# Grouped-query attention on one core: the first queries in one transposed load, all plain loads of the first groups at the top

## The chip, the cores and the metric

One NeuronCore of a Trainium2 chip runs the whole problem. The metric is the device time of the execution in microseconds, the median over several executions.

## The reference

```python
B, Hq, Hkv, Sq, Sk, D = 16, 32, 8, 288, 512, 128          # bf16, q, k, v ~ 0.05 * normal

def reference(q, k, v):
    k = jnp.repeat(k, rep, axis=1); v = jnp.repeat(v, rep, axis=1)      # rep = 4
    scores = jnp.einsum("bhqd,bhkd->bhqk", q, k) * D ** -0.5
    p = softmax(scores, axis=-1)
    return jnp.einsum("bhqk,bhkd->bhqd", p, v)
```

## The kernel before

There are 128 groups (batch times key head). Each has 1152 query rows (nine tiles of 128), 512 keys, and three **rounds**, so 384 rounds. A round's scores are 1536 columns of PSUM in three blocks of 512 (the kernel's `BANK`): TensorE makes the transposed scores, ScalarE takes the exponential, TensorE multiplies with the values two rounds later, VectorE divides. Scores and exponentials alternate between two halves of PSUM.

Queries and most keys come by transposed loads that SyncE issues. For a quick start the keys of groups 0 and 1 come by plain loads that ScalarE issues and are transposed on TensorE; the queries of group 0 come in two transposed loads, of four and five tiles.

```python
def op_q0(i):                                   # two loads: tiles 0..3 and 4..8
    c0, c1 = ((0, TB), (TB, NT))[i]
    nc.sync.dma_start_transpose(qt_sb[:, 0, c0:c1], q_v[0:P, c0 * D:c1 * D]).then_inc(sem["s_qp%d" % i], 16)

def have_q(g, i):
    if g == 0:
        return ("s_qp%d" % min(i, 1), 16)       # round 0: first half; rounds 1, 2: second half
    ...

first = [lambda i=i: op_q0(i) for i in range(2)]
first += [lambda: op_q(1), lambda: op_k(0, 2), lambda: op_v(0, None, 1, UG), lambda: op_q(2), lambda: op_q(3)]

@block.tensor
def _(eng):
    op_warm(WARM, BANK, ps_o[:, 1])             # WARM = 5 dummy matmuls of 512 columns
    op_warm(1, P, ps_o[:, 1])
    op_kt(0, range(1), 0)                       # transposes of group 0's keys
    op_kt(0, range(1, NJ), 1)
    op_warm(1, P, ps_s[:, 1])
    for n in range(NS):
        op_s(n)                                 # scores of round n
        if shared(n):
            op_sy(n)
        if n == 2:
            op_kt(1, range(NJ), 1)              # transposes of group 1's keys
        if n >= LAG:
            op_pv(n - LAG)                      # values of round n - 2
    ...

@block.scalar
def _(eng):
    op_kd(eng, 0)                               # keys of group 0
    eng.activation(dum[:], nc.const_aps.tensor(0.0, [P, 1], FP32), ACTF.Exp)     # fetches the table (1.28 us)
    for (s, n) in need(eng, [("s_kd0", 16)]):
        eng.wait_ge(s, n)                       # until they have landed
    op_v(0, eng, 0, 1)                          # values of group 0
    op_kd(eng, 1)                               # keys of group 1
    for n in range(NS):
        op_exp(n)                               # rounds 0 and 1 in three pieces of 512 columns
    ...
```

In every sixth round (`shared`) the last 120 columns of the exponential are computed on VectorE.

## Time and profile before

| | before |
|---|---|
| time, median of 3 | 522.29 us (522.13, 522.29, 523.44) |
| span of the profiled execution | 521.9 us, and that execution took 523.58 us |
| TensorE / ScalarE busy | 99% / 98% |
| first half of group 0's queries | issued 0.82, landed 3.6 us |
| second half | issued 2.20, landed 6.53 us |
| first exponential of round 0 / 1 | 4.42 / 7.22 us |
| scores of round 3 begin | 10.35 us |

Read it from the head: what happens after round 3 is a gap-free stream, so the start of that stream, plus a constant, is the time.

### The profile page before, as it was taken

How to read it: one execution, taken by the hardware profiler on the slowest of the kernel's cores; microseconds unless marked ns; L12 is line 12 of the kernel's file. 1: busy time of each engine (PE TensorE's matmuls, PEld its weight loads, DVE VectorE, ACT ScalarE, POOL GpSimd, SP SyncE). 2: the span in 40 equal slices, each digit the busy share in tenths (PEclk: the TensorE clock that was granted, in tenths of full speed). 3: DMA queues.
4: the chain of work that ended last, by engine and by line, in shares of the span. 5: the costliest groups of instructions: out<-in, count | busy, mean ns of one | idle time of the engine just before them, and what ended most of it. 6: DMA issues, size and time to landing. Idle time of an engine off the chain costs nothing.

```text
span 521.9 us, 15338 instructions
## 1 busy us (share of the span) xinstructions
PE 517.0 (99%) x6223; PEld 395.2 (76%) x6223; DVE 368.2 (71%) x1307; ACT 513.7 (98%) x393; POOL 79.8 (15%) x135
## 2 busy tenths in 40 slices
PE   8999999999999999999999999999999999999997
PEld 4777777777777777777777777777777777777776
DVE  1777677677677777776776766767767777677675
ACT  6999999999999999999999999999999999999997
POOL 2111111111111111111111111111111111111110
PEclk9999999999999999999999999999999999999999
DMA  8999999999999999999999989999999999998212
GB/s 181 243 228 234 217 209 217 245 208 232 224 219 270 187 251 200 229 257 226 224 229 239 179 233 231 226 202 193 218 248 232 214 215 195 197 244 183 91 69 92
DMA packets 253110, 110.06 MB, mean 211 GB/s; under 512 B 219760, under 2 KB 236784, under 8 KB 253040
## 3 DMA queue, kind: packets, MB, share of 16 engines
q1 hardware_dynamic: 252608, 108.69, 97.2%
q8 instruction: 49, 0.80, 0.6%
q10 hardware_dynamic: 432, 0.39, 0.3%
q14 instruction: 21, 0.17, 0.1%
HBM read 17.04 MB, written 37.75 MB: 105 GB/s over the span
## 4 chain that ended last, share of the span: by engine, by line
ACT 97%; PE 1%; DMA 1%; issue 1%; DVE 0%; SPq 0%
ACT pt_sb L514 96%; DMA qt_sb<-in_q_dram 1%; PE ps_s L437 1%; SPq L316 0%; ACT pt_sb L509 0%; PE ps_o L477 0%; DVE o_sb L583 0%; PE ps_o L404 0%; DVE o_sb L593 0%; PE ps_s L477 0%; DVE rl_sb L573 0%; PE ps_o L667 0%; DVE bad_sb L619 0%; DVE flag_i L733 0%; DVE bad_sb L616 0%
## 5 line engine op out<-in xcount | busy, mean ns | idle before, releaser
L514 ACT ACTIVATE pt_sb<-ps_s 128x1536 bf16<-128x1536 f32 (+2 forms) x384 | 509.2, 1441 | 0.9 <-PE ps_s L437 0.9
L477 PE MATMUL ps_o<-v_sb,pt_sb 128*128 128x129 bf16 x4584 | 322.2, 220 | 0.0
L477 PEld LDWEIGHTS ps_o<-v_sb,pt_sb 128*128 128x128 bf16 x4584 | 283.0, 98 | 49.7 <-DVE o_sb L583 13.7
L437 PE MATMUL ps_s<-qt_sb,kt_sb 128*128 128x512 bf16 (+2 forms) x1536 | 310.9, 325 | 1.3 <-DMA qt_sb<-in_q_dram 1.3
L583 DVE TENSOR_TENSOR o_sb<-ps_o,rl_sb 128x384 bf16<-128x384 f32 x382 | 211.9, 555 | 9.3 <-DVE rl_sb L573 0.5
L437 PEld LDWEIGHTS ps_s<-qt_sb,kt_sb 128*128 128x128 bf16 x1536 | 124.1, 98 | 64.1 <-DMA qt_sb<-in_q_dram 2.5
L573 DVE RECIPROCAL rl_sb<-ps_o 128x3 f32<-128x3 f32 x382 | 68.0, 178 | 126.8 <-PE ps_o L477 125.3
L566 POOL COPY v_sb<-vd_sb 128x512 bf16<-128x512 bf16 x128 | 78.9, 616 | 430.9 <-PE ps_o L477 418.7
L547 DVE SCALAR_TENSOR_TENSOR u_sb<-u_sb,m_sb 128x120 f32<-128x120 f32 x124 | 35.1, 283 | 2.1
L554 DVE SCALAR_TENSOR_TENSOR pt_sb<-u_sb,e_sb 128x120 bf16<-128x120 f32 x62 | 17.5, 283 | 2.2
L547 DVE SCALAR_TENSOR_TENSOR u_sb<-m_sb 128x120 f32<-128x120 f32 x62 | 17.1, 276 | 0.0
L525 DVE TENSOR_SCALAR y_sb<-ps_o 128x120 f32<-128x120 f32 x62 | 15.7, 253 | 0.0
L538 DVE TENSOR_SCALAR m_sb<-t_sb 128x120 int32<-128x120 int32 x62 | 13.8, 223 | 2.1
L448 PE MATMUL ps_o<-qt_sb,kt_sb 128*128 128x120 bf16 x62 | 13.4, 216 | 0.0
L538 DVE TENSOR_SCALAR e_sb<-t_sb 128x120 int32<-128x120 int32 x62 | 13.4, 216 | 0.0
L531 DVE TENSOR_SCALAR t_sb<-y_sb 128x120 int32<-128x120 f32 x62 | 13.2, 212 | 0.0
L448 PEld LDWEIGHTS ps_o<-qt_sb,kt_sb 128*128 128x128 bf16 x62 | 6.1, 98 | 7.3
L411 DVE COPY kt_sb<-ps_o 128x128 bf16<-128x128 bf16 (+2 forms) x3 | 1.0, 336 | 8.2 <-PE ps_o L404 8.1
L509 ACT ACTIVATE pt_sb<-ps_s 128x512 bf16<-128x512 f32 x6 | 3.3, 627 | 2.9 <-PE ps_s L437 2.9
L609 DVE TENSOR_REDUCE st_sb<-rl_sb 128x1 f32<-128x72 f32 (+1 forms) x16 | 3.5, 216 | 0.0
L611 DVE TENSOR_REDUCE st_sb<-rl_sb 128x1 f32<-128x72 f32 (+1 forms) x16 | 3.5, 216 | 0.0
L417 PE MATMUL ps_o<-const-bfloat16-1.0 128*128 128x512 bf16 (+1 forms) x6 | 2.4, 573 | 0.9 <-PEq L751 0.9
(32 smaller groups left out, 12.5 us busy)
## 6 DMA issues: line engine op xcount, KB each, us to landing
out_dram<-o_sb SPq DMA_DIRECT2D x127, 288.0 KB, 3.8
vd_sb<-in_v_dram SPq DMA_DIRECT2D x31, 512.0 KB, 5.3
qt_sb<-in_q_dram SPq DMA_TRANSPOSE x129, 5.0
kt_sb<-in_k_dram SPq DMA_TRANSPOSE x32, 5.0
vd_sb<-in_v_dram SPq DMA_DIRECT2D x1, 384.0 KB, 3.9
out_dram<-o_sb SPq DMA_DIRECT2D x3, 96.0 KB, 1.6
kd_sb<-in_k_dram ACTq DMA_DIRECT2D x2, 128.0 KB, 2.8
vd_sb<-in_v_dram ACTq DMA_DIRECT2D x1, 128.0 KB, 2.4
```

The costliest lines, as they stand in the source:

```text
L437: ins = emit(eng, w_x, lambda: eng.matmul(ps_s[:, n % 2, c:c + w], kt_sb[:, sl, j, gi, :], qg[:, t * P:t * P + w], start=True, stop=True))
L448: emit(eng, [("s_ev", n - LAG - 1)], lambda: eng.matmul(ps_o[:, (n - LAG) % 2, BANK - W:BANK], kt_sb[:, (g // UG) % NSLOT, j, g % UG, :], ...
L477: ins = emit(eng, w_x, lambda: eng.matmul(outs(r)[:, t - r % NC * TPC, :], pt(g, t, j), v_sb[:, sl, gi * NJ + j, 0:DV], start=(x == 0), st ...
L514: emit(eng, waits, lambda: eng.activation(d, s, ACTF.Exp, scale=scale)).then_inc(sem["s_e"], 1)
L525: emit(eng, [("s_yb", nth(n) - NB), ("s_pv", n - LAG + 1)], lambda: eng.tensor_scalar(out=y_sb[:, b], in0=ps_o[:, (n - LAG) % 2, BANK - W: ...
L531: emit(eng, [("s_ym", 2 * (nth(n) - NB)), ("s_y", nth(n))], lambda: eng.tensor_scalar(out=t_sb[:, b], in0=y_sb[:, b], scalar1=Y_MUL, scala ...
L538: emit(eng, [("s_yp", nth(n) - NB), ("s_yb", nth(n))], lambda: eng.tensor_scalar(out=dst[:, b], in0=t_sb[:, b], scalar1=mask, scalar2=bits ...
L547: lambda: eng.scalar_tensor_tensor(out=u_sb[:, b, x], in0=src, scalar=QUARTIC[x], in1=m, op0=ALU.add, op1=ALU.mult)
L554: lambda: eng.scalar_tensor_tensor(out=pt_sb[:, n % NPT, CH - W:CH], in0=u_sb[:, b, 2], scalar=QUARTIC[3], in1=e_sb[:, b].bitcast(FP32), o ...
L566: emit(eng, waits, lambda: eng.tensor_copy(v_sb[:, sl, gi * NJ:(gi + 1) * NJ, 0:D], vd_sb[:, sl, gi].rearrange("p (j d) -> p j d", d=D))). ...
L573: emit(eng, [("s_pv", r + 1)], lambda: eng.reciprocal(rl_sb[:, TPC * r:TPC * (r + 1)].unsqueeze(2), outs(r)[:, :, D:DV])).then_inc(sem["s_ ...
L583: emit(eng, waits, lambda: eng.tensor_tensor(out=o_sb[:, g % NO, t0:t0 + TPC, :], in0=outs(r)[:, :, 0:D], in1=rl_sb[:, TPC * r:TPC * (r + ...
```

## The change

The intent is a shorter head: one issue on SyncE less, so that the queries of group 1 follow at once, and no wait on ScalarE ahead of its second and third load.

```diff
-            c0, c1 = ((0, TB), (TB, NT))[i]
+            c0, c1 = 0, NT
...
-                return ("s_qp%d" % min(i, 1), 16)
+                return ("s_qp0", 16)
...
+                if n == 1 and x < 2:
+                    w_x = [have_q(g, x)]
...
-            return FIRST_SHARED <= n < NS - 6 and (n - FIRST_SHARED) % EVERY == 0
+            return FIRST_SHARED <= n < NS - NC and (n - FIRST_SHARED) % EVERY == 0
...
-        first = [lambda i=i: op_q0(i) for i in range(2)]
+        first = [lambda: op_q0(0)]
...
-        sp.append((NS - 2 + LAG + 2.5, op_stored))
+        sp.append((NS - NC + LAG + 2.5, op_stored))
...
-                if n == 2:
+                if n == 1:
                     op_kt(1, range(NJ), 1)
...
             op_kd(eng, 0)
-            eng.activation(dum[:], nc.const_aps.tensor(0.0, [P, 1], FP32), ACTF.Exp)
-            for (s, n) in need(eng, [("s_kd0", 16)]):
-                eng.wait_ge(s, n)
             op_v(0, eng, 0, 1)
             op_kd(eng, 1)
+            eng.activation(dum[:], nc.const_aps.tensor(0.0, [P, 1], FP32), ACTF.Exp)
```

NC is 3, so the new limit in `shared` adds one shared round, number 378. The transposes of group 1's keys move from behind scores 2 to behind scores 1.

## The prediction

> **What bounds the kernel now.** I read the engine shares of the page first, then busy time by stretches, then the order of time on TensorE, then the chain that ended last for the first 20 us. The page puts the chain on ScalarE (96% of the span in the exponentials), but two engines are nearly full there:
>
> ```profile
> PE 517.0 (99%) x6223; PEld 395.2 (76%) x6223; DVE 368.2 (71%) x1307; ACT 513.7 (98%) x393; POOL 79.8 (15%) x135
> ```
>
> The busy time of stretches (columns: PE, PEld, DVE, ACT, POOL, granted clock, DMA share, GB/s) and the order of time in the middle decide which one leads:
>
> ```profile
> 200.00:300.00 100.00, 100.00 (x1219) 76.96 (x1218) 73.14 (x262) 100.00 (x77) 15.51 (x26) 1.00 1.08 229
> ...
> 31.63 0.81 PE L437 MATMUL ps_s<-qt_sb,kt_sb 128*128 128x512 bf16 x3
> 32.28 0.84 PE L477 MATMUL ps_o<-v_sb,pt_sb 128*128 128x129 bf16 x12
> 32.96 0.82 PE L437 MATMUL ps_s<-qt_sb,kt_sb 128*128 128x512 bf16 x6
> ```
>
> The reader is to see starts, not lengths, because matmuls overlap: scores to values 0.65 us, values to the next scores 0.68 us, so 1.33 us for one of the 384 rounds, without a gap. ScalarE keeps up by a hair. Every sixth round its exponential is 120 columns short because VectorE computes them. While that goes on, its durations stay between 1390 and 1477 ns; after the last such round (502.1 us) they creep up, which I read as a queue building:
>
> ```profile
> L514 ACT ACTIVATE pt_sb<-ps_s x7: 1390/1452/1477, 29.8 to 37.8; 128x1536 bf16<-128x1536 f32 x6, 128x1416 bf16<-128x1416 f32 x1
> ...
> L514 ACT ACTIVATE pt_sb<-ps_s x11: 1391/1478/1540, 502.1 to 515.4; 128x1536 bf16<-128x1536 f32 x10, 128x1416 bf16<-128x1416 f32 x1
> ```
>
> So from about 11 us to 515 us TensorE's stream has no slack and nothing in this change shortens it. All that can move is the head and a little of the tail. The chain of the head:
>
> ```profile
> 0.82 1.32 SPq L316
> 2.14 0.06 issue
> 2.20 4.33 DMA qt_sb<-in_q_dram
> 6.53 0.05 issue
> 6.57 2.74 PE ps_s L437 x9
> 9.31 0.43 PE ps_o L404 x4
> 9.74 0.70 PE ps_o L477 x12
> 10.44 0.73 PE ps_s L437 x3
> ```
>
> The end of the time is set by the second half of the queries of group 0: issued at 2.20, landed at 6.53. The first half lets round 0 run (3.79 to 5.2), then TensorE sits idle for 1.34 us. Since no slack follows, each microsecond taken off this head comes off the total.
>
> [...] (1) [...] a 512-column matmul lasts 634 ns at most in the head and 379 ns in the middle, starts 0.43 us apart there and 0.215 us (0.65/3) here; the fast spacing comes at about 9.5 us, 3.0 us after TensorE became busy without a gap. The granted-clock column shows 1.00 in both and does not tell them apart. (2) [...] loads issued by different engines share the same 16 DMA engines. The trace agrees: in 4.5 to 5.0 us the queue of ScalarE's loads takes 86.5% of them and the queue of SyncE's transposes 7.5%. (3) [...] SyncE's queue moved 0.17 MB from 3 to 5 us, about all of its 0.16 MB, yet it landed only at 6.53, when ScalarE's loads (issued 3.07 and 3.44) were still draining. [...]
>
> ```profile
> L437 PE MATMUL ps_s<-qt_sb,kt_sb x9: 314/607/634, 6.6 to 9.0; 128*128 128x512 bf16 x5, 128*128 128x128 bf16 x4
> ...
> L437 PE MATMUL ps_s<-qt_sb,kt_sb x25: 219/379/379, 30.7 to 38.7; 128*128 128x512 bf16 x15, 128*128 128x128 bf16 x8, 128*128 128x392 bf16 x2
> ...
> q10 hardware_dynamic: 151, 0.14, 86.5%
> q1 hardware_dynamic: 49, 0.00, 7.5%
> ```
>
> **The change, part by part.**
>
> *One transposed load for group 0.* Removed: one issue of about 1.3 us on SyncE. The nine-tile issues of the other groups take 1391 to 1857 ns, median 1639, hardly more than four or five tiles (1319, 1255). So the single issue runs from 0.82 to about 2.45, and everything behind it in SyncE's queue comes 2.20 + 1.25 - 2.45 = 1.0 us sooner. In the kernel before, bytes began to flow when an issue was about over (second half: issue over at 3.45, first bytes at about 3.55), so I put them at 2.5.
>
> *Plain loads without the wait.* ScalarE's three loads go out at 0.82, about 1.25 and about 1.6 instead of 0.82, 3.07, 3.44. Their bytes (3 x 131 KB = 0.39 MB) start at 1.8 as the first does now, and compete with the 0.295 MB of queries. Both queues at their best moved 0.14 MB in half a microsecond, 0.28 MB per us (queries in 6.5 to 7.0, plain in 4.5 to 5.0). My estimate: (0.39 + 0.295) / 0.28 = 2.45 us from 1.8, so all bytes through at 4.25. The first half's bytes ended at about 3.1 and it landed at 0.82 + 2.8 = 3.6, so I add 0.5: 4.75. I choose **4.9** for the landing T of the queries, as the second half had a stall on top (ScalarE's queue busy 71% for only 0.06 MB in 5.0 to 5.5).
>
> *The table load after the issues.* It moves from 1.23 to about 2.05 and ends, with its dummy, at about 3.55. Round 0's exponential cannot start before T + 0.6. Off the path: 0.
>
> *Order on TensorE.* Before, the path after 6.53 is scores 1, scores 2, the four transposes of group 1's keys, values 0, then scores 3 at 10.3. After, it is scores 0, scores 1, transposes, scores 2, values 0, scores 3, all behind T. At full rate a score round costs 0.65, the transposes 0.22 (half of the 0.43), values 0.68. Work before: 0.65 + 0.65 + 0.22 + 0.68 = 2.2; after: 2.85. If d is the time at half rate after becoming busy, d/2 is lost in both. Before: 6.53 + 2.2 + 3.0/2 = 10.23, and the trace has 10.3 (a small wait for the copy of group 1's keys fills the rest, and goes away with the earlier transposes). After: 4.9 + 2.85 + 1.5 = 9.25. So the head wins 10.3 - 9.25 = **1.05 us**. ScalarE does not stop this: exponentials of rounds 0 and 1 take 1.57 us each in thirds and fit under two half-rate score rounds (1.28 each) and the transposes.
>
> *Shared round 378, waits for stores earlier.* A share puts the ScalarE's duration back by about 87 ns (1477 to 1390), so the last exponential ends about 0.08 us sooner. The check of old stores moves ahead of a store that waits for later data anyway: 0. Queries right behind, earlier by 1 us: nobody waited for them: 0.
>
> Sum: 1.05 + 0.08 = 1.1 us of 522.29; I write 521.3, shaded a little for stalls.
>
> **Rivals.** *The single load lands late* (a transfer that crowds another). For it: three plain loads now run beside it[...]. Against it: the total bytes are small, and all start 1 to 2 us sooner. Break-even is where T + 0.65 = 6.53, that is T = 5.9; at T = 6.5 the time would be 522.8. [...] Each further microsecond at half rate costs 0.5 us; but the kernel before has the same gamble, so this mainly widens the range (its three runs lie 1.3 us apart). *ScalarE becomes the bound of the head* through the late table load: it would need T below 3.0; nothing would be lost against before. *A wait takes its place further on* (group 1's keys or queries): its keys now arrive with the first loads, and its queries' issue ends at about 4.1, landing by about 6.5 against a need at T + 4.3 = 9.2. Against it; it would cost a few tenths. *Hidden anyway*: refuted by the gap-free middle.
>
> **Range and chances.** T between 4.65 and 5.6 gives a gain of 1.35 down to 0.4 us; [...] I take 520.5 to 522.4. A 2% change is 10.4 us, more than the whole head to the first steady round, so faster or slower by that much would take something that the profile does not show: 1% each.
>
> **What would show it right or wrong.** One query load at L316, landing 4 to 4.8 us after its issue; TensorE's wait for queries before round 0 longer, the one of 1.34 us before round 1 gone; the first exponential later (5.5 instead of 4.42) but scores 3 at 9.2 to 9.9 instead of 10.3; the steady exponentials 1.0 us earlier at the same place in the order; durations of the last exponentials staying below 1480 ns. A landing after 5.9, a head that ends at 11 us still, or a middle with gaps would make it wrong.

## The result, and the profile after

| | executions, us | median |
|---|---|---|
| before | 522.29, 523.44, 522.13, 523.5 | 522.87 |
| after | 522.23, 522.48, 523.57, 522.38 | 522.43 |
| before, all 27 executions | 14 from 521.94 to 522.39 (mean 522.22), 13 from 523.24 to 523.86 (mean 523.66) | 522.39 |
| after, all 10 | 522.15 to 524.7 (mean 522.98) | 522.66 |

The ratio of the first pair is 0.9997, with a 95% interval of 0.9974 to 1.0019. (Ratios are the mean time of one kernel's fast runs over that of the other's of the same rounds, so not quite the ratio of the medians.) The predicted gain of about a microsecond is missing, and the median lies just above the stated range. The kernel before has **two clusters** of times, 1.4 us apart, about half of the executions in each.

The chain of the head after, in order of time (start us, length us, what; L439 are the scores, L511 and L516 the exponentials), answers to the chain of the head shown in the prediction:

```profile
0.82 4.42 DMA qt_sb<-in_q_dram
5.25 0.05 issue
5.29 0.41 PE ps_s L439
5.70 0.02 issue
5.72 1.08 ACT pt_sb L511 x2
6.81 0.49 ACT pt_sb L516
```

The reader is to see that the chain leaves TensorE after one matmul and stays on ScalarE. Before, it ran over TensorE until 11.17. The score matmuls of the same stretch say why. They run at the short length of the middle (379 ns; "full rate" from here on), not at the 634 ns of the head before ("half rate"; starts 0.43 us apart there, 0.215 us in the middle), so TensorE is at full rate when the queries land:

```profile
L439 PE MATMUL ps_s<-qt_sb,kt_sb x12: 219/380/391, 5.3 to 7.5; 128*128 128x512 bf16 x8, 128*128 128x128 bf16 x4
```

From there on TensorE waits for ScalarE, and not the other way round (waited for: us in total, times, longest). In the same window of the kernel before, no matmul waits for an exponential:

```profile
PEld ps_s L439 <- ACT pt_sb L516: 0.8, 2, 0.4
PE ps_o L479 <- ACT pt_sb L516: 0.5, 1, 0.5
```

Most of the signs that the prediction named for being right are there: the queries land 4.42 us after their issue, the first exponential is at 5.72, the wait before round 1 is gone, the last exponentials stay near 1480 ns, and scores 3 begin at 8.27, before the forecast 9.2 to 9.9. The gain did not come with them.

And the tail of the exponentials, answering to the 1391/1478/1540 before:

```profile
L516 ACT ACTIVATE pt_sb<-ps_s x10: 1394/1452/1481, 502.2 to 514.2; 128x1536 bf16<-128x1536 f32 x9, 128x1416 bf16<-128x1416 f32 x1
```

The span is 520.5 us and that execution took 522.23, against 521.9 and 523.58. It looks like a gain of 1.35 us. But an execution at full rate was compared with one at half rate. What the two kernels do at the **same** rate of TensorE is what the experiments had to find out.

### The profile page after: what moved, and what is told of

It reads as the page before. It is cut to its first block, busy times and chain, and to the rows that moved or that the text cites. A ratio compares the mean times of both kernels' runs of the same rounds, so it can differ in the third digit from the quotient of the medians.

```text
span 520.5 us, 15349 instructions
## 1 busy us (share of the span) xinstructions
PE 515.2 (99%) x6224; PEld 394.2 (76%) x6224; DVE 369.6 (71%) x1315; ACT 513.3 (99%) x393; POOL 79.4 (15%) x135
## 4 chain that ended last, share of the span: by engine, by line
ACT 98%; DMA 1%; issue 1%; DVE 0%; PE 0%
ACT pt_sb L516 97%; DMA qt_sb<-in_q_dram 1%; ACT pt_sb L511 1%; DVE o_sb L585 0%; DVE o_sb L595 0%; PE ps_s L479 0%; PE ps_s L439 0%; DVE rl_sb L575 0%; PE ps_o L669 0%; DVE bad_sb L621 0%; DVE flag_i L733 0%; DVE bad_sb L618 0%
## 5 line engine op out<-in xcount | busy, mean ns | idle before, releaser
L516 ACT ACTIVATE pt_sb<-ps_s 128x1536 bf16<-128x1536 f32 (+2 forms) x384 | 508.8, 1443 | 0.0
L439 PE MATMUL ps_s<-qt_sb,kt_sb 128*128 128x512 bf16 (+2 forms) x1536 | 309.4, 324 | 1.2 <-DMA qt_sb<-in_q_dram 1.2
L439 PEld LDWEIGHTS ps_s<-qt_sb,kt_sb 128*128 128x128 bf16 x1536 | 123.6, 98 | 62.7 <-DMA qt_sb<-in_q_dram 1.5
L511 ACT ACTIVATE pt_sb<-ps_s 128x512 bf16<-128x512 f32 x6 | 3.3, 618 | 2.0 <-PE ps_s L439 2.0
```

What stands on the lines that cost most here:

```text
L439: ins = emit(eng, w_x, lambda: eng.matmul(ps_s[:, n % 2, c:c + w], kt_sb[:, sl, j, gi, :], qg[:, t * P:t * P + w], start=True, stop=True))
L516: emit(eng, waits, lambda: eng.activation(d, s, ACTF.Exp, scale=scale)).then_inc(sem["s_e"], 1)
```

## The experiments

Twelve runs. The theory after the first traces: in the lower cluster TensorE comes to full rate early in the head, in the upper one late; and at full rate ScalarE, not TensorE, paces the head. Each run has one profile; what its other executions did is known from their times alone.

### 1. Fill TensorE's idle gap in the kernel before

```diff
                 op_s(n)
+                if n == 0:
+                    op_warm(3, BANK, ps_s[:, 1])
```

> The kernel before, with three more 512-column dummy matmuls on TensorE between scores 0 and scores 1, where it sat idle for 1.34 us. Theory 1 (the two clusters of times, 522.2 and 523.5, [...] at full rate early, or at half rate until about 9.5 us): [...] the upper cluster goes away: all runs at 522.1 to 522.5, scores 1 at full rate or full rate from about 6 us on. Theory 2 (the clusters have nothing to do with the head, e.g. transfers or the chip's state): two clusters stay, 522.2 and 523.5, as in the kernel before.

Measured: 522.3, 522.26, 522.06, 522.21, 522.2. The upper cluster is gone, while the kernel before, in the same rounds, had five of eleven executions in it. Five executions without the upper cluster would come by chance about once in 25 times; together with runs 3 and 4, where the lower cluster is gone, this ties the clusters to TensorE's rate in the head. Why filling brings the full rate sooner, no run shows. This run also shows the head of the kernel before with full rate from about 6.5 us (378 ns at the median from 6.4 to 8.9; L437 are scores, L417 the filling, L509 and L514 exponentials), which the first profile could not:

```profile
5.24 1.28 PE ps_s L417 x3
6.52 0.45 PE ps_s L437
6.97 0.02 issue
6.99 1.09 ACT pt_sb L509 x2
8.08 4.33 ACT pt_sb L514 x4
```

From 6.99 on, round 1's exponentials run without a gap on ScalarE. Round 0's were over long before, in the wait for the second half of the queries. In the timeline of the changed kernel the same exponentials of round 1 start later than that, although its queries had all landed at 5.25 instead of 6.36:

```profile
7.17 1.11 ACT L511 ACTIVATE pt_sb<-ps_s 128x512 bf16<-128x512 f32 x2
```

### 2. Fill the gap in the changed kernel

```diff
-            op_warm(1, P, ps_s[:, 1])
+            op_warm(3, BANK, ps_s[:, 1])
```

> The changed kernel, with three 512-column dummy matmuls in place of the one small one that stands ahead of scores 0, so that TensorE is busy from 0.8 us to the landing of the queries at about 5.25. Theory 1 [...]: no run near 523.5 any more; all at 522.1 to 522.5, since at full rate ScalarE sets the pace from the first exponential on. Theory 2: one run in four still at 523.5.

Measured: 522.89, 522.58, 522.84, 523.48, 522.39, 524.0. Missed: TensorE was at full rate in the profile (379 ns), but the times did not fall together. The profile shows another source of spread: the single load landed 5.1 us after its issue, at 5.92, not at 5.25; the first exponential started at 6.39 instead of 5.72, and the span was 521.2 instead of 520.5. The 0.67 us of the landing came through in full (0.7).

### 3 and 4. No warm-up matmuls in either kernel

```diff
-    WARM = 5
+    WARM = 0
```

> The changed kernel without its five 512-column warm-up matmuls. Theory 1: TensorE is at half rate until about 9.5 us in every run; all times in the upper cluster, 523.4 to 524.0; in the profile scores 0 to 2 at 634 ns for 512 columns [...]. Theory 2: same two clusters as before.

> The kernel before without its five warm-up matmuls. Theory 1: all times in the upper cluster, 523.4 to 524.0. If the time at which full rate comes is the same in both kernels (about 9.5 us[...]), the two kernels without warm-up are equal within 0.2 us; if it comes 3 us after TensorE became busy without a gap, as the prediction took it, the changed one is about 1 us faster.

Measured: changed kernel 523.23 to 524.42, mean 523.84; kernel before 523.37 to 525.12, mean 523.98. No execution of either at 522.2, as theory 1 wants, though the spread is wider than the expected 523.4 to 524.0; the difference of 0.14 us is within the scatter. The chains, changed kernel first:

```profile
5.31 2.74 PE ps_s L439 x6
8.05 0.43 PE ps_o L404 x4
8.48 1.13 PE ps_s L439 x6
9.63 4.01 ACT pt_sb L516 x3
```

```profile
6.75 2.74 PE ps_s L437 x9
9.49 0.43 PE ps_o L404 x4
9.92 0.80 PE ps_o L477 x12
```

At half rate two rounds of scores cost 2.74 us in either kernel, and here TensorE does pace the head. The full rate came at about 9.2 us in the one profile and at about 10.0 in the other: neither at one fixed time nor 3.0 us after TensorE became busy (3.9 and 3.3). Both of the alternatives for run 4 are too simple; the time varies, and what sets it no run shows.

### 5. Put ScalarE's wait back

```diff
             op_kd(eng, 0)
+            eng.activation(dum[:], nc.const_aps.tensor(0.0, [P, 1], FP32), ACTF.Exp)
+            for (s, n) in need(eng, [("s_kd0", 16)]):
+                eng.wait_ge(s, n)
             op_v(0, eng, 0, 1)
             op_kd(eng, 1)
-            eng.activation(dum[:], nc.const_aps.tensor(0.0, [P, 1], FP32), ACTF.Exp)
```

> The changed kernel with ScalarE's wait put back: its second and third load go out only when the keys of group 0 have landed (about 3.0 us), and the table load stands ahead of them again. Theory A (the three plain loads crowd the queries' load): the 0.295 MB of queries has the DMA engines nearly to itself from 2.3 to about 3.5 us and lands at about 4.2; first exponential at about 4.7 instead of 5.72; since at full rate every time so far was the first exponential plus 514.8 us, the span is about 519.5 and the time about 521.2. Theory B (a nine-tile transposed load takes 4.4 us by itself, as those of the other groups do): landing at 5.2 again, time 522.3, no change.

Measured: 522.06 to 523.45, mean 522.67; landing at 5.20 us. Theory A failed: the queries land no sooner when the two other plain loads go out at 3.15 and 3.52. Nor do those loads crowd the end of the queries' load: in the trace, ScalarE's queue moves nothing between 3.0 and 5.3 us. What runs beside the queries there is SyncE's own next load, the queries of group 1, issued at 2.26. (This profile was at half rate, 634 ns.)

### 6. Two loads again, all plain loads at the top

```diff
-            c0, c1 = 0, NT
+            c0, c1 = ((0, TB), (TB, NT))[i]
...
-                return ("s_qp0", 16)
+                return ("s_qp%d" % min(i, 1), 16)
...
-        first = [lambda: op_q0(0)]
+        first = [lambda i=i: op_q0(i) for i in range(2)]
```

> The changed kernel with the queries of group 0 in two transposed loads again (all else as changed, with a finer wait: round 1 begins with a piece that needs the first half alone). Theory A (crowding): the first half lands later than the 3.59 of the kernel before, at about 4.2, the second at about 5.3, with no wait between exponentials 0 and 1 of over 0.3 us; first exponential at about 5.0, time 521.5. Theory B: the first half lands at 3.6 as before; time about 521.2. If the single load was right and the two loads cost an issue of 1.3 us on the path, time 522.3 or more.

Measured: 522.45 to 523.38, mean 522.95. The first half landed 4.07 us after its issue (4.90), against 2.8 in the kernel before with the same load: beside three plain loads even four tiles are late by 1.3 us. By what means the plain loads hold it up, no run shows. So the waits of the kernel before protected its first half, and the plain loads at the top by themselves bring nothing. The expected first exponential at 5.0 came at 5.59.

### 7. Two loads, the late plain loads held for the first half

```diff
             (as in 6, and on ScalarE:)
             op_kd(eng, 0)
+            eng.activation(dum[:], nc.const_aps.tensor(0.0, [P, 1], FP32), ACTF.Exp)
+            for (s, n) in need(eng, [("s_qp0", 16)]):
+                eng.wait_ge(s, n)
             op_v(0, eng, 0, 1)
             op_kd(eng, 1)
-            eng.activation(dum[:], nc.const_aps.tensor(0.0, [P, 1], FP32), ACTF.Exp)
```

> Two query loads as in the run above, and ScalarE's second and third load held until the first half of the queries has landed (3.6 us). Theory A: first half at 3.6, second half free of the plain loads at about 5.1; first exponential at 4.42, round 1 follows it with a gap under 0.3 us; span 4.42 + 514.8 + 0.3 = 519.5 at most, time 521.0 to 521.3, the best of all. Rival: values and keys of group 1 now come too late (landing 6.0 to 6.8), TensorE waits for them ahead of values 0 or scores 3, and the time stays at 522.2.

Measured: 522.07 to 524.0, mean 522.95. The first part of the expectation held (first half at 3.55, second at 5.07, 2.9 us after its issue against 4.3 in the kernel before; round 1 right behind round 0), and the rival took all of it: the transposes of group 1's keys, which the change had moved up, stood ahead of scores 2 and waited for a load that landed at 8.04 us:

```profile
3.94 4.10 DMA kd_sb<-in_k_dram
8.04 0.05 issue
8.08 0.40 PE ps_o L404 x4
```

### 8. The added shared round taken out

```diff
-            return FIRST_SHARED <= n < NS - NC and (n - FIRST_SHARED) % EVERY == 0
+            return FIRST_SHARED <= n < NS - 6 and (n - FIRST_SHARED) % EVERY == 0
```

> The changed kernel with the shared round 378 taken out again. The last exponentials' durations climb to about 690 to 710 ns as in the kernel before, instead of 627 to 653, and the span minus the start of the first exponential is 514.87 instead of 514.78; the single time says nothing.

The durations of the last exponentials came as expected, first without the share, then the changed kernel with it:

```profile
L511 ACT ACTIVATE pt_sb<-ps_s x2: 688/692/697, 518.2 to 518.7; 128x512 bf16<-128x512 f32 x2
```

```profile
L511 ACT ACTIVATE pt_sb<-ps_s x2: 627/634/640, 515.5 to 516.0; 128x512 bf16<-128x512 f32 x2
```

That is 58 ns less at the medians, of the predicted size of under 0.1 us. What it takes off the whole time is too small for the times to show. The expected 514.87 us from the first exponential to the end was missed: the span of 523.3 minus 6.75 is 516.55, because this execution was at half rate until about 11.7 us. With a landing at 6.06 on top it took 524.96 us. That one execution shows how bad the head of the changed kernel can get when both chances go against it.

### 9. The changed kernel, five rounds more

No edit.

> The changed kernel itself, five rounds more, since the verdict so far rests on four runs. What is to be explained is why about a microsecond of gain is missing. If the prediction's mechanism held and the first four runs were bad luck, the median lies near 521.3. By the theory formed from the runs so far (at full rate ScalarE paces the head from the landing T of the single load: time = T + 517; T varies from 5.2 to 6.1; at half rate another 1 to 2.5 us) the times spread from 522.2 to 524.5 without two clear clusters, none under 522.1.

Measured: 522.96, 522.61, 522.15, 522.71, 524.7, 524.02. No two clusters, none near 521.3. Its profiled execution (522.96 us, span 521.3) was at half rate, so it can be held against the profile of the kernel before, which was too:

```profile
0.82 4.73 DMA qt_sb<-in_q_dram
5.55 0.05 issue
5.60 2.74 PE ps_s L439 x6
8.34 0.34 PE ps_o L404 x4
8.68 0.67 PE ps_s L439 x6
```

Here the prediction's sum fits. With the landing at 5.55 and full rate from about 8.35 (d = 2.75 us, read from the same trace), scores 3 should start at 5.60 + 2.85 + 2.75/2 = 9.83; they did at 9.85, against 10.35 before. The span is 0.6 us shorter (521.3 against 521.9). But scores 3 are not what the end waits for in this profile either: after the last line shown the chain goes over to ScalarE at 9.37 and stays there, and round 3's exponential starts at 10.72, when ScalarE is free (11.19 before, when it waited 0.39 us for scores 3).

### 10. The kernel before, filled, with round 0 made to wait for both halves

```diff
-                    w_x = [("s_k0", 1), waits[1]] if x == 0 else waits[:1]
+                    w_x = [("s_k0", 1), ("s_qp1", 16), waits[1]] if x == 0 else waits[:1]
...
-            op_warm(1, P, ps_s[:, 1])
+            op_warm(6, BANK, ps_s[:, 1])
```

(and without the filling of run 1 after scores 0; the filling now stands ahead of scores 0). No transfer changes; only what must wait for the second half.

> The kernel before with filled TensorE, in which scores 0 also wait for the second half of the queries, as they have to with the single load; transfers unchanged. Theory A (round 0's three exponentials of 0.48 us each, which the two loads hide in the wait for the second half, come behind the landing and ScalarE cannot catch up): the second half lands at 6.4, first exponential at about 6.9, round 1's at 8.3 instead of 6.99; time 523.2 to 523.6, that is 1.0 to 1.4 us over the 522.21 of the filled kernel without this wait. Theory B (TensorE paces the head, as the prediction took it): only scores 0 (0.65 us at full rate) come behind the landing: time 522.5 to 522.9.

Measured: 523.62, 523.8, 523.78, 523.79, 522.96, 523.67, mean 523.60, against 522.21 of run 1: 1.4 us more, as theory A says and far from theory B's 0.3 to 0.7. (Run 1 ran on the other chip; the lower cluster of the kernel before averages 522.26 there and 522.18 here, so the chip is not the difference.) The chain:

```profile
2.20 4.19 DMA qt_sb<-in_q_dram
6.39 0.14 issue
6.53 0.39 PE ps_s L437
6.92 0.02 issue
6.94 1.09 ACT pt_sb L509 x2
8.03 0.49 ACT pt_sb L514
```

The first exponential starts at 6.94, where in run 1 round 1's did. All of round 0's exponential (three pieces, starts 0.48 to 0.49 us apart, 1.45 together) has come behind the landing. TensorE's 0.65 us of scores hardly count. This is the cost of a single load, measured by itself: at full rate it must land 1.4 us sooner than the second half did, only to come out even. In the changed kernel it landed 1.1 us sooner (5.25 against 6.36), or 0.4 us (5.92, run 2).

### 11. The queries' load with one plain load beside it

```diff
             (on ScalarE, as in 7: the second and third load wait for the queries)
-                if n == 1:
-                    op_kt(1, range(NJ), 1)
                 if n >= LAG:
                     op_pv(n - LAG)
+                if n == 2:
+                    op_kt(1, range(NJ), 1)
```

> The changed kernel with ScalarE's second and third load held until the queries of group 0 have landed, and the transposes of group 1's keys moved behind values 0 so that they hold nothing up. It measures the landing of the nine-tile load with only one plain load beside it. Theory A (plain loads hold the landing back): T between 3.9 and 4.4, against 5.25 in the changed kernel and 5.20 with the wait for the keys. Theory B (the transposed load takes that long by itself): T at 5.0 or later. The time then says how much of it survives the late values and keys of group 1: 521.4 if nothing is lost again, 522.3 if a new wait takes it.

Measured: landing at 4.95 us, just under theory B's bound of 5.0 and far from A's 3.9 to 4.4. The chain:

```profile
0.82 4.13 DMA qt_sb<-in_q_dram
4.95 0.02 issue
4.97 3.88 DMA vd_sb<-in_v_dram
```

So about 4.1 us is what the nine tiles need with only the keys of group 0 as a plain load beside them. Run 5 is a second measure of the same: there too nothing else of ScalarE's moved before the landing, which came at 5.20. With all three plain loads at the top it came at 5.25, 5.27, 5.55, 5.92 and 6.06: two of the five are within 0.07 us of that second measure, so the crowding by plain loads is shown at most for the later three. In all these runs the transposed load of group 1's queries follows at 2.26 in SyncE's queue, 1.25 us sooner than in the kernel before; whether it holds the landing back was not tested. The time, 524.12 to 524.52, is lost again to the values that now land at 8.85.

### 12. Run 7, with the late keys out of the way of scores 2

Run 7 with the transposes of group 1's keys behind values 0 (the last edit of run 11).

> The run with two query loads and late plain loads, with the transposes of group 1's keys behind values 0 instead of behind scores 1, where TensorE had waited 2.2 us for the keys with scores 2 queued behind. Theory: exponential 2 follows 1 at about 7.3, values 0 at about 7.4, and the wait for group 1's keys (landing about 8.0) now holds up scores 3 only: exponential 3 at about 9.4 against 10.5, span 520.0, time about 521.7 in the fast phase. Rival: the keys' wait just moves, exponential 3 at 10.3 or later, time 522.5 as before.

Measured: 522.35, 521.97, 522.09, 521.9, 522.32, 521.55, median 522.03, ratio to the kernel before 0.9981 (0.9965 to 0.9998). It has the lowest mean (522.03); the filled kernel of run 1 (522.21, ratio 0.9985, 0.9969 to 1.0001) is steadier. Neither has an execution in the upper cluster. The further 0.2 us over run 1 is not shown as a gain: the runs are from two chips, and in the profiles run 12 is no faster (span 520.7 against 520.6). The expected 521.7 was not reached by the median: exponential 3 came at 9.98, not 9.4, because the keys' path was longer than I had it:

```profile
8.20 0.34 PE ps_o L404 x4
8.54 0.02 issue
8.56 0.43 DVE kt_sb L411
9.00 0.14 issue
9.13 0.82 PE ps_s L439 x3
```

The copy on VectorE and the handover after the transposes (0.6 us together) stand ahead of scores 3.

## Why the prediction was wrong

**Which execution was read.** The prediction read its gain from the profile of before and subtracted it from 522.29. But that profile belongs to an execution of 523.58 us, of the half-rate cluster, and 522.29 is of the full-rate cluster. The step that failed first is "the kernel before has the same gamble, so this mainly widens the range". The gamble is how long TensorE stays at half rate. Run 1 shows that it separates two different critical paths: at full rate the chain of the kernel before leaves TensorE at 6.97, and there is no TensorE time left to win in its head.

**"ScalarE does not stop this"** is the step of the mechanism that failed. It rests, as it says, on exponentials that "fit under two half-rate score rounds". At half rate they do fit, by less than 0.1 us (run 9: round 1's exponential ends at 9.29, scores 2 at 9.35). At full rate a score round takes 0.65 us and an exponential in pieces 1.43 to 1.45, and ScalarE paces everything from the landing on. The prediction counted only scores 0 (0.65 us) as new work behind the landing, and took for hidden the exponential of round 0, which the two loads hide in the wait for the second half. Run 10 prices it: 1.4 us. ScalarE as the bound of the head stood among the rivals, but only for a late table load.

**The landing T.** Put at 4.9 us, it was 5.25, 5.27, 5.55, 5.92 and 6.06 in the five profiles with this head (after, runs 3, 9, 2, 8). The sum counted the bytes of all three plain loads, and still came out as low as the load with one of them beside it (4.95 and 5.20, runs 11 and 5). For that case the same sum would have said 1.8 + (0.131 + 0.295)/0.28 + 0.5 = 3.8 us. So the term that is off is not the bytes of the plain loads but what else a nine-tile load costs; which part of it, the runs do not separate. The late landing I did name, as the first rival, with a break-even at 5.9; two of the five profiles reach it.

**Slips that decided nothing.** Scores 3 began at 10.35 before, not 10.3. Of ScalarE's two later loads only the one issued at 3.44 was still on its way at 6.53 (landed 6.76); the other had landed at 5.48. The exponentials in pieces take 1.57 us from start to end but follow each other every 1.45, as they overlap.

**The steps that held.** At half rate the sum over TensorE gives the start of scores 3 to 0.02 us once T and d are read from the trace (run 9), and the span is 0.6 us shorter. The added shared round shortens the last exponentials by about 0.06 us each (run 8). The table load (1.28 us, ended at 3.5) is off the path.

**The sum.** At full rate the change moves the wait for the second half into one behind the single load: from even (522.23 after, 522.22 before) to 0.7 us worse (run 2). At half rate the profiles say a gain of about 0.6 us (T = 5.55, run 9; spans of 521.5 and 522.2 in runs 3 and 4), but the six executions each of runs 3 and 4, all at half rate as far as the times tell, differ by only 0.14 us on the mean, so this gain is not established. Added to these are late times (524.0 in run 2, 524.02 and 524.7 in run 9, 524.96 in run 8). Only the last has a profile, and there a late landing (6.06) and a late full rate coincide; for the others this is a guess, and for run 2, whose gap was filled, a poor one. The means over all executions, 522.98 and 522.91, are equal within their scatter. What stays open: why the landing varies by 0.8 us from one execution to another with the same loads at the head, and what sets the time at which full rate comes (from before 5.3 to about 11.7 us in the profiles). How often the changed kernel runs at half rate is known only from its profiles.

## What to carry to other kernels

Look at the single executions, not at their median alone: here two clusters, 1.4 us or 0.3% apart, meant two critical paths, and a profile shows only one of them, so ask first which one it was taken from. The rate of TensorE decided which engine paced the head: at 634 ns for a matmul of 512 columns TensorE (2.74 us for two rounds of scores), at 379 ns ScalarE (1.43 to 1.45 us for an exponential in pieces, against 0.65 us for a round of scores). A load cut in two is not only latency: here it let ScalarE work through the first piece in the wait for the second, and the single load had to beat the second piece's landing by all of that work (1.4 us, run 10). Giving TensorE dummy work in a gap of its head was worth 0.7 us on the mean here, with five executions within 0.24 us; the one rearrangement of the loads that helped, run 12, was worth 0.9.

The landing times of the transposed loads, with SyncE's next transposed load following each: 2.7 to 2.8 us for four tiles (before, runs 1, 7, 10, 12) and 4.1 to 4.4 us for nine (runs 11, 5) with one plain load of 128 KB beside them; 4.1 us for four (run 6) and 4.4 to 5.2 us for nine (after, runs 2, 3, 8, 9) beside three such loads.
